# Attention, gated feed-forward and adaptive layer norm on one core: scores with keys on partitions, no row maximum, token-major projections, one pool layout

## Chip, cores, metric

One core of one Trainium2 chip. The time is the device time of one execution in microseconds (us), the median of several. A core has five engines that matter here: TensorE (PE; its weight loads, PEld, overlap its matmuls), VectorE (DVE), ScalarE (ACT), GpSimd (POOL, used here to issue transfers) and SyncE (SP, which issues most DMA transfers). SBUF is the memory that holds the tiles, PSUM the one that matmul results go to.

## The reference, cut to what matters

```python
S, D, Hq, Hkv, Dh, W, F = 2048, 1024, 32, 4, 128, 512, 3584       # batch 1, bfloat16
mod = (silu(c) @ w_mod).reshape(1, 6, 1, -1)                      # sa ca ga sb cb gb
h = layernorm(x) * (1 + ca) + sa
q = (h @ wq) per head;  k, v = last W rows of the caches, each shared by 8 heads
p = softmax(q @ k.T * Dh ** -0.5)                                 # 2048 x 512, per head
x = x + ga * ((p @ v), heads side by side) @ wo
h = layernorm(x) * (1 + cb) + sb
x = x + gb * ((silu(h @ w_gate) * (h @ w_up)) @ w_down)
```

The tokens are worked on in 4 chunks of 512. With 32 heads this makes 128 "heads" (a head of a chunk). Counted in matmuls with a moving operand of 512 columns, the reference needs 1024 for q, 512 for scores, 512 for p @ v, 1024 for wo and 2688 for the feed-forward part: 5760 in all.

## The kernel before

It puts queries on partitions for the scores, so that the row maximum and the row sum are reductions along the free axis. Then P must be transposed for p @ v; that is done by matmuls with a diagonal of the reciprocal sums. The residual x is kept feature-major (`xT`), so the final output is transposed back. The parts that the change touches, with cuts:

```python
def emit_q(g):                       # 8 matmuls, then qT (128 x 512) copied by ScalarE
    ...
def emit_s(g, qt):                   # qt: four blocks of 128 queries
    s_ps = aps_s.tile([P, W], FP32, name="s_ps", tag="s_ps")
    nc.tensor.matmul(s_ps, lhsT=st[g]["qT"][:, qsl], rhs=kT[:, kv, :], start=True, stop=True)
def emit_max(g, qt):
    nc.vector.tensor_reduce(out=mx, in_=s_ps, axis=AX.X, op=ALU.max)
    nc.vector.tensor_scalar(out=nmx, in0=mx, scalar1=-scale, scalar2=None, op0=ALU.mult)
def emit_exp(g, qt):
    nc.scalar.activation(out=p_sb, in_=s_ps, func=ACT.Exp, bias=st[g]["nmx"][qt],
                         scale=scale, accum_out=ssum)
def emit_recip_dg(g, qt):
    nc.vector.reciprocal(out=rs, in_=ssum)
    nc.vector.tensor_scalar(out=dg, in0=ident, scalar1=rs, scalar2=None, op0=ALU.mult)
def emit_T(g, qt):                   # P transposed and normalised by matmuls with dg
    for j in range(WT):
        nc.tensor.matmul(pT_ps[:, j, :], lhsT=p_sb[:, j * P:(j + 1) * P], rhs=dg, ...)
    (nc.vector.tensor_copy or nc.scalar.copy)(out=pT4[:, qt, :, :], in_=pT_ps)
def emit_o(g):                       # 4 matmuls with v_sb, copied by VectorE
    ...
# output projection: for a column block of 128, 32 matmuls with wo as stationary operand
nc.tensor.matmul(a_ps, lhsT=wo_t[:, hh, :], rhs=oT_bufs[cc][hg][:, hi, :], ...)
# second layer norm, feature-major: sums over features by matmuls with ones
nc.tensor.matmul(ln_ps[:, 0, :], lhsT=ones_bf, rhs=srcT[:, dt, ssl], ...)
nc.tensor.matmul(ln_ps[:, 1, :], lhsT=ones_bf, rhs=xsq, ...)
nc.scalar.activation(out=var_all, in_=var_all, func=ACT.Ln)
nc.scalar.activation(out=rstd, in_=var_all, func=ACT.Exp, scale=-0.5)
# end of a chunk: xf (features on partitions) transposed to tokens, copied, stored
nc.tensor.transpose(o_ps[:, dt, :], xf[:, dt, qt * P:(qt + 1) * P], ident)
```

The program text is not the order of execution: when it is built, a scheduler orders each engine's instructions and gives out the buffers.

## Time and profile before

| | before |
|---|---|
| median (lowest to highest), us | 1562.4 (1561.97 to 1566.34) |
| span of the profiled execution, us | 1565.7 |
| start to the first query projection | 65.2 |
| heads, output projection, second norm | 887.1 |
| feed-forward part and end | 613.4 |

The page's busy times of the kernel before (busy us, share of the span, instructions):

```profile
span 1565.7 us, 22987 instructions
## 1 busy us (share of the span) xinstructions
PE 1484.2 (95%) x8370; PEld 738.9 (47%) x8528; DVE 964.8 (62%) x2865; ACT 790.3 (50%) x1797; POOL 17.5 (1%) x31
```

A table of the kernel before by stretches of time: for each stretch its length, busy time and instruction count of each engine, the granted TensorE clock (1.00 is full), the DMA share and GB/s. The cuts are at the first query projection and the first gate matmul.

```profile
core 0: us, PE busy (x) PEld busy (x) DVE busy (x) ACT busy (x) POOL busy (x), PEclk, DMA share, GB/s
0.00:65.20 65.20, 41.41 (x337) 30.27 (x338) 41.82 (x130) 38.69 (x48) 3.47 (x9) 0.85 0.65 194
65.20:952.30 887.10, 851.29 (x5270) 437.78 (x5371) 732.44 (x2450) 661.87 (x1612) 5.29 (x6) 0.99 0.41 85
952.30:1565.70 613.40, 591.48 (x2768) 270.90 (x2821) 190.56 (x286) 89.75 (x139) 8.70 (x16) 0.99 0.57 148
```

TensorE is busy nearly all the time, but busy time alone does not say how many matmuls a head costs. The timeline does. Three successive p @ v groups of the kernel before (start, duration, engine, line, operation, output<-inputs, shape, count):

```profile
391.28 1.03 PE L413 MATMUL o_ps<-pT_6158,v_sb 128*128 128x512 bf16 x4
...
397.64 1.03 PE L413 MATMUL o_ps<-pT_6263,v_sb 128*128 128x512 bf16 x4
...
404.00 0.81 PE L413 MATMUL o_ps<-pT_6370,v_sb 128*128 128x512 bf16 x3
```

They start 6.36 us apart. A head has 24 matmuls of 512 columns (8 q, 4 scores, 4 p @ v, 8 wo) and 16 of 128 columns for the transposes. At 0.2162 us (39.8 us for 184 matmuls in a stretch of the feed-forward part) the 24 take 5.19 us; the transposes take the rest, 1.17 us. One matmul is listed with 379 ns while starts are 216 ns apart: the listed durations of neighbours overlap, so the distance between starts is what counts.

The costliest groups (line, engine, operation, shapes, count, busy us, mean ns, idle before):

```profile
L367 ACT ACTIVATE p_sb<-s_ps,nmx 128x512 bf16<-128x512 f32 x512 | 353.0, 699 | 4.4 <-DVE nmx L359 0.7 <-DVE rs L376 0.2
L357 DVE TENSOR_REDUCE mx<-s_ps 128x1 f32<-128x512 f32 x512 | 337.4, 682 | 19.0 <-PE s_ps L350 15.7 <-PE q_ps L334 0.2
...
L399 PE MATMUL pT_ps<-dg,p_sb 128*128 128x128 bf16 x2048 | 182.1, 218 | 12.9 <-ACT pT_8030 L404 2.4 <-ACT pT_11517 L404 2.4 <-ACT pT_872 L404 0.7
```

The exponentials and the row maxima look most expensive. They lie on engines with room, except among the heads before the output projection begins (65 to 268 us). One slice, in the form of the table above:

```profile
160.00:200.00 40.00, 36.57 (x247) 18.66 (x249) 38.76 (x142) 38.28 (x96) 0.00 (x0) 1.00 0.24 54
```

The third of the costliest lines is on the engine that binds.

### The profile page before, as it was taken

What the parts mean: (1) busy time and instruction counts of PE and PEld (TensorE: products, weight loads), DVE (VectorE), ACT (ScalarE), POOL (GpSimd) and SP (SyncE); (2) the same over time, 40 slices, a digit from 0 to 9 for tenths busy, and PEclk for the clock granted to TensorE, in tenths of its full rate; (3) what the DMA queues carried; (4) which work ended last, traced back from release to release, by engine and by line L of the source; (5) the groups of instructions that cost most, each with busy time, mean ns of one, the idle gap of its engine ahead of it and who ended that gap; (6) DMA issues with size and microseconds to landing.
All of it is one profiled execution on the core that took longest, in us unless ns stands there. A gap on an engine that the chain in (4) does not pass through costs nothing.

```text
span 1565.7 us, 22987 instructions
## 1 busy us (share of the span) xinstructions
PE 1484.2 (95%) x8370; PEld 738.9 (47%) x8528; DVE 964.8 (62%) x2865; ACT 790.3 (50%) x1797; POOL 17.5 (1%) x31
## 2 busy tenths in 40 slices
PE   6799999999999999999999999999999999999997
PEld 4544444555554555554555544444444444444443
DVE  5678999888888988888888715331333134213421
ACT  4658999777778877779777605110111011001100
POOL 0010000000000000000000000000000000000000
PEclk9799999999999999999999999999999999999998
DMA  8356222343534343434342477447645755574434
GB/s 272 62 167 133 54 55 48 68 95 72 97 73 84 68 95 68 95 68 89 74 95 48 81 135 208 162 161 141 168 143 166 138 158 161 155 142 154 141 71 98
DMA packets 452434, 178.71 MB, mean 114 GB/s; under 512 B 385760, under 2 KB 447200, under 8 KB 452320
## 3 DMA queue, kind: packets, MB, share of 16 engines
q1 hardware_dynamic: 448832, 164.64, 45.4%
q0 software_dynamic: 3488, 12.59, 2.3%
q8 instruction: 66, 1.08, 0.3%
q14 instruction: 48, 0.39, 0.1%
HBM read 173.02 MB, written 4.19 MB: 113 GB/s over the span
## 4 chain that ended last, share of the span: by engine, by line
PE 60%; issue 21%; ACT 10%; DVE 6%; DMA 1%; another core or an unknown queue 0%; POOL 0%; SPq 0%; ACTq 0%; POOLq 0%; DVEq 0%
PE a_ps L435 13%; PE q_ps L334 8%; PE d_ps L563 6%; PE g_ps L545 6%; PE u_ps L549 6%; PE s_ps L350 6%; PE pT_ps L399 6%; PE o_ps L413 5%; ACT p_sb L367 3%; DVE mx L357 2%; PE row_ps L221 2%; DMA xg_114<-in_A_x_dram 1%; PE modT_ps L230 1%; ACT qT L337 1%; DVE dg L386 1%
## 5 line engine op out<-in xcount | busy, mean ns | idle before, releaser
L367 ACT ACTIVATE p_sb<-s_ps,nmx 128x512 bf16<-128x512 f32 x512 | 353.0, 699 | 4.4 <-DVE nmx L359 0.7
L357 DVE TENSOR_REDUCE mx<-s_ps 128x1 f32<-128x512 f32 x512 | 337.4, 682 | 19.0 <-PE s_ps L350 15.7
L552 ACT ACTIVATE sig<-g_ps 128x512 bf16<-128x512 f32 x112 | 66.8, 597 | 444.0 <-PE g_ps L545 432.5
L399 PEld LDWEIGHTS <-p_sb 128*128 128x128 bf16 x2048 | 146.8, 97 | 124.4 <-issue 61.4
L563 PE MATMUL d_ps<-guT,wd 128*128 128x512 bf16 x879 | 195.3, 379 | 1.3 <-DMA wd<-in_B_w_down_dram 0.3
L399 PE MATMUL pT_ps<-dg,p_sb 128*128 128x128 bf16 x2048 | 182.1, 218 | 12.9 <-ACT pT_8030 L404 2.4
L350 PE MATMUL s_ps<-kT,qT 128*128 128x512 bf16 x506 | 160.7, 380 | 4.0 <-ACT p_sb L367 1.7
L435 PEld LDWEIGHTS <-wo_t 128*128 128x128 bf16 x1024 | 100.3, 98 | 122.4 <-issue 6.3
L563 PEld LDWEIGHTS <-wd 128*128 128x128 bf16 x896 | 87.5, 98 | 104.5 <-DMA wd<-in_B_w_down_dram 0.8
L549 PEld LDWEIGHTS <-wu 128*128 128x128 bf16 x896 | 87.4, 98 | 103.7 <-issue 0.8
L545 PEld LDWEIGHTS <-wg 128*128 128x128 bf16 x896 | 87.5, 98 | 103.2 <-issue 1.1
L565 DVE SCALAR_TENSOR_TENSOR xf<-d_ps,modT,xT 128x512 bf16<-128x512 f32 x32 | 24.0, 751 | 181.1 <-PE d_ps L563 181.1
L386 DVE TENSOR_SCALAR dg<-ident,rs 128x128 bf16<-128x128 bf16 x512 | 122.4, 252 | 6.1
L334 PEld LDWEIGHTS <-wq_h 128*128 128x128 bf16 x1024 | 90.4, 99 | 48.6 <-issue 4.2
L376 DVE RECIPROCAL rs<-ssum 128x1 f32<-128x1 f32 x512 | 81.5, 159 | 47.0 <-ACT p_sb L367 36.4
L367 ACT ACTIVATION_READ_ACCUMULATOR p_sb<-s_ps,nmx 128x1 f32 x512 | 109.3, 214 | 0.0
L413 PEld LDWEIGHTS <-v_sb 128*128 128x128 bf16 x512 | 48.8, 98 | 73.2 <-DVE nmx L359 11.0
L337 ACT CAST qT<-q_ps 128x512 bf16<-128x512 f32 x128 | 76.2, 595 | 4.8 <-PE q_ps L334 4.8
L350 PEld LDWEIGHTS <-qT 128*128 128x128 bf16 x512 | 49.5, 98 | 57.3 <-issue 3.6
L359 DVE TENSOR_SCALAR nmx<-mx 128x1 f32<-128x1 f32 x512 | 72.6, 142 | 0.0
L334 PE MATMUL q_ps<-h1T_106,wq_h 128*128 128x512 bf16 x241 | 71.4, 388 | 0.7 <-issue 0.2
L334 PE MATMUL q_ps<-h1T_109,wq_h 128*128 128x512 bf16 x242 | 68.8, 383 | 0.7
(815 smaller groups left out, 1910.6 us busy)
## 6 DMA issues: line engine op xcount, KB each, us to landing
wq_h<-in_A_wq_dram SPq DMA_DIRECT2D x128, 256.0 KB, 2.9
wo_t<-in_A_wo_dram SPq DMA_DIRECT2D x32, 1024.0 KB, 6.6
wg<-in_B_w_gate_dram SPq DMA_DIRECT2D x28, 1024.0 KB, 5.3
wu<-in_B_w_up_dram SPq DMA_DIRECT2D x28, 1024.0 KB, 7.2
wd<-in_B_w_down_dram SPq DMA_DIRECT2D x32, 896.0 KB, 5.8
wm_l<-in_w_mod_dram POOLq DMA_DIRECT2D x8, 1024.0 KB, 6.2
wm<-in_w_mod_dram SPq DMA_DIRECT2D x4, 1024.0 KB, 6.4
out_dram<-o_sb POOLq DMA_DIRECT2D x16, 256.0 KB, 2.3
```

The lines of the kernel that those rows point to most:

```text
L334: nc.tensor.matmul(q_ps, lhsT=wq_h[:, dt, :], rhs=h1T[cc][:, dt, :], start=(dt == 0), stop=(dt == DT - 1))
L337: nc.scalar.copy(out=qT, in_=q_ps)
L350: nc.tensor.matmul(s_ps, lhsT=st[g]["qT"][:, qsl], rhs=kT[:, kv, :], start=True, stop=True)
L357: nc.vector.tensor_reduce(out=mx, in_=s_ps, axis=AX.X, op=ALU.max)
L367: nc.scalar.activation(out=p_sb, in_=s_ps, func=ACT.Exp, bias=st[g]["nmx"][qt], scale=scale, accum_out=ssum)
L386: nc.vector.tensor_scalar(out=dg, in0=ident, scalar1=rs, scalar2=None, op0=ALU.mult)
L399: nc.tensor.matmul(pT_ps[:, j, :], lhsT=p_sb[:, j * P:(j + 1) * P], rhs=dg, start=True, stop=True)
L413: nc.tensor.matmul(o_ps, lhsT=v_sb[:, kv, j, :], rhs=pT4[:, :, j, :], start=(j == 0), stop=(j == WT - 1))
L435: nc.tensor.matmul(a_ps, lhsT=wo_t[:, hh, :], rhs=oT_bufs[cc][hg][:, hi, :], start=(hh == 0), stop=(hh == H - 1))
L545: nc.tensor.matmul(g_ps, lhsT=wg[:, dt, fi * P:(fi + 1) * P], rhs=hsrc[:, dt, :], start=(dt == 0), stop=(dt == DT - 1))
L549: nc.tensor.matmul(u_ps, lhsT=wu[:, dt, fi * P:(fi + 1) * P], rhs=hsrc[:, dt, :], start=(dt == 0), stop=(dt == DT - 1))
L563: nc.tensor.matmul(d_ps, lhsT=wd[:, f, :], rhs=guT[:, f, :], start=(f == 0), stop=(f == FT - 1))
```

## The change

Intent: put keys on partitions for the scores. P then comes out of the exponential in the layout that p @ v needs, and the transposes go. The row maximum would now be a reduction over partitions. It is left out; instead the chip computes a bound on the scores from norms of weights and keys, and if it is exceeded a branch at the end runs the old code ("general path"). Row sums come from adding the four key blocks on VectorE and one matmul with ones; the reciprocal is exp(-ln(sum)) on ScalarE, from one activation table set. The output and down projections have tokens on partitions, so the residual stays token-major and the last transposes go. Weights come in 512-column blocks. All SBUF tiles share a few pools. The core of the diff, with cuts:

```diff
+def emit_s(g):
+    p = blkA("pT", [P, WT, TCW])
+    for jj in range(WT // 2):
+        s_ps = big("s_ps")                                # 128 x 2 x 512, two PSUM banks
+        for i in range(2):
+            j = 2 * jj + i
+            nc.tensor.matmul(s_ps[:, i, :], lhsT=kT[:, kv, j * P:(j + 1) * P], rhs=qT[g], ...)
+        nc.scalar.activation(out=p[:, 2 * jj:2 * jj + 2, :], in_=s_ps, func=ACT.Exp, scale=scale)
+    nc.vector.tensor_tensor(out=a, in0=p[:, 0:2, :], in1=p[:, 2:4, :], op=ALU.add)
+    nc.vector.tensor_tensor(out=b, in0=a[:, 0, :], in1=a[:, 1, :], op=ALU.add)
+def emit_o(g):
+    nc.tensor.matmul(l_ps, lhsT=ones_bf, rhs=rec.pop(g), start=True, stop=True)
+    for j in range(WT):
+        nc.tensor.matmul(o_ps, lhsT=v_sb[:, kv, j, :], rhs=pT[g][:, j, :], ...)
+    nc.scalar.activation(out=r, in_=l_ps, func=ACT.Ln)
+    nc.scalar.activation(out=r, in_=r, func=ACT.Exp, scale=-1.0)
+    nc.vector.tensor_tensor(out=oT[(cc, hg)][:, hi, :], in0=o_ps, in1=r, op=ALU.mult)
+def emit_wo(cc, q, u):                                    # tokens on partitions, 8 heads at a time
+    nc.tensor.matmul(a_ps, lhsT=oT[(cc, 2 * q + i)][:, hh % 4, t * P:(t + 1) * P],
+                     rhs=wo_tiles[(cc, q, dh, i)][:, hh % 4, :], ...)
+def ln_stats(key, cc):                                    # per row of x, then 32 transposes to hT
+    for t in range(QT):
+        for i in range(DH):
+            nc.vector.bn_stats(out=st[:, i, :], in_=xt[cc * QT + t][:, i * 512:(i + 1) * 512])
+        nc.vector.bn_aggr(out=mv[:, t, :], in_=st)
+    nc.scalar.activation(out=rstd, in_=mv[:, :, 1], func=ACT.Ln, bias=eps_t)
+    nc.scalar.activation(out=rstd, in_=rstd, func=ACT.Exp, scale=-0.5)
+nc.scalar.preload_act_table_set("natural_log_exp_and_others")
+def bound_wq(hg, i, j): ...                               # 32 sums of squares over wq, one per head
+def bound_k(): ...
+def bound_final(): ...                                    # sets flag
+def emit_down(cc, dh, t):                                 # tokens on partitions, stored at once
+    nc.tensor.matmul(d_ps, lhsT=guT[(cc, f // 4)][:, f % 4, t * P:(t + 1) * P],
+                     rhs=wd_tiles[(cc, dh, f // 4)][:, f % 4, :], ...)
 ...
+    fast_path(tc, flag, *args)
+    over = nc.values_load(flag[0:1, 0:1], min_val=0, max_val=1)
+    with tc.If(over > 0):
+        general_path(tc, *args)
```

## The prediction

> **What bounds the kernel now.** TensorE. The page's busy table has PE at 95% of 1565.7 us, VectorE 62%, ScalarE 50%. In the feed-forward part (952 us to the end) a table by stretches gives 184 matmuls of 512 columns in 39.8 us: 0.2162 us each, with no gaps to speak of at granted clock 1.00. The Trainium skill (TensorE: Matmul & The Clock Gate, Back-to-back issue gap) gives 216 ns for one gap at 512 columns, which agrees; its "sustained 131 ns" does not. In attention the timeline shows a steady head every 6.36 us: 24 such matmuls (5.19 us) plus 16 transposing matmuls of 128 columns for P (about 1.17 us). Only the first 32 heads differ: before output-projection work arrives (65 to 268 us) VectorE (97% busy) and ScalarE (96%) bind, through the row maximum (682 ns each), exp with bias and accumulator read (699 + 214 ns), reciprocals, diagonal scalings and PSUM copies. The prologue ends at 65 us, where the first query projection starts.
>
> **Removed.** The 2048 transposing matmuls (about 1.17 us a head, 150 us of PE), 512 row maxima, negations, reciprocals, diagonals and 512 copies of transposed P. On the critical path that is the PE part, plus the vector/scalar excess of the early heads. The x-transposes of the prologue, the mean/variance matmuls with ones (some 27 us) and the final output transposes (about 14 us with their waits) go too.
>
> **Added.** One matmul a head for the row sums (0.216 us); 256 normalisation transposes (0.065 us, as the warm ones in the trace: 17 us); modulation columns (256 tiny matmuls, estimate 0.06 us) and 32 broadcast matmuls; VectorE sums of P, the bound check (32 products over weights, estimate 1.2 us each, hidden) and ScalarE's logarithm and exponential per head. ScalarE per head: two 1024-wide exps at about 1.02 us (the 1024-wide copy takes that) plus two of 0.6: 3.3 us. VectorE: 3 to 4.5 us. Both are under PE's 25 x 0.2162 = 5.41 us, so PE stays the limit.
>
> **Sum (us).** Prologue about 33 (6 MB at the 272 GB/s of the first slice, then modulation columns), was 65. Nine heads without projection work: limited by the chain scores, exps, sums, query copy, about 4.6 each plus the key bound: 46. 119 heads at 5.41, with the 1% that clock dips cost: 650. Modulation and broadcasts 12, normalisation transposes 13, stalls where eight statistics (0.66 us) jam VectorE and so exp, about 12. Projection left after the last head 16, last normalisation 7. Feed-forward 2688 x 0.2162 = 581, plus dips and waits for second-half down weights: 592. Tail with the branch 7. Total 1388.
>
> **Prediction: 1388 us, 1350 to 1430; faster by over 2% 0.97, within 2% 0.02, slower 0.01.**
>
> **What would show it.** Steady heads 5.4 us apart; first query projection near 33 us; VectorE and ScalarE under 80% throughout; feed-forward within 2% of 600 us; a few microseconds lost near each normalisation's statistics; no table loads between logarithm and exponential.
>
> **What would make it wrong.** Before, each Ln and the Exp after it cost a table load of 1.28 us; the skill (ScalarE: Activation LUTs, Table sets) says one set holds both, and the change preloads it. If loads nevertheless come twice a head, ScalarE needs 5.9 us a head and binds: about 1460. Larger stalls at normalisations or chained engine waits within a head (0.5 us a head is 64 us), or down weights arriving late, push it above 1430; a prologue overlapped better and no stalls give 1350.

## The result, and the profile after

| | before | after |
|---|---|---|
| median (lowest to highest), us | 1562.4 (1561.97 to 1566.34) | 1340.36 (1339.75 to 1341.4) |
| start to the first query projection | 65.2 | 26.9 |
| heads, output projection, second norm | 887.1 | 720.6 |
| feed-forward part and end | 613.4 | 591.3 |
| span of the profiled execution | 1565.7 | 1338.8 |

The ratio is 0.8562 (95% interval 0.8541 to 0.8583). The change was forecast in direction and kind; the time fell 48 us under the forecast and 10 us under the lower end of its range.

The busy line of the changed kernel:

```profile
span 1338.8 us, 15768 instructions
## 1 busy us (share of the span) xinstructions
PE 1302.6 (97%) x6332; PEld 604.0 (45%) x6457; DVE 670.0 (50%) x1208; ACT 486.4 (36%) x654; POOL 18.1 (1%) x38
```

The same table by stretches, cut at the same two events of the changed kernel:

```profile
core 0: us, PE busy (x) PEld busy (x) DVE busy (x) ACT busy (x) POOL busy (x), PEclk, DMA share, GB/s
0.00:26.90 26.90, 9.18 (x177) 7.77 (x178) 10.50 (x35) 4.93 (x9) 0.69 (x6) 0.84 0.94 298
26.90:747.50 720.60, 713.94 (x3497) 331.52 (x3565) 524.52 (x969) 410.25 (x528) 0.00 (x0) 0.99 0.36 117
747.50:1338.80 591.30, 579.52 (x2666) 264.67 (x2719) 135.02 (x205) 71.22 (x117) 17.41 (x32) 0.99 0.44 145
```

A steady head of the changed kernel on TensorE (timeline):

```profile
151.44 1.89 PE L945 MATMUL a_ps<-wo,oT 128*128 128x512 bf16 x8
153.17 0.38 PE L922 MATMUL l_ps<-psB,ones_bf 128*128 128x512 bf16 x1
153.38 1.03 PE L925 MATMUL o_ps<-pT,v_sb 128*128 128x512 bf16 x3
154.25 1.03 PE L903 MATMUL s_ps<-qT,kT 128*128 128x512 bf16 x4
155.11 1.89 PE L888 MATMUL q_ps<-hT,wq 128*128 128x512 bf16 x8
156.84 1.89 PE L945 MATMUL a_ps<-wo,oT 128*128 128x512 bf16 x8
```

From 151.44 to 156.84 are 5.40 us (three heads in a row: 5.395) for 8 + 1 + 4 + 4 + 8 = 25 matmuls, that is 0.2158 us each (the "x3" has lost one record). No line shows a wait. The list of TensorE's waits over the whole execution is short (who waited for whom, us in total, times, longest):

```profile
PE sil_ps L721 <- DVE sil_r L719: 8.0, 1, 8.0
PE k_ps L816 <- DMA k_ld<-in_A_k_cache_dram: 6.3, 1, 6.3
PE h_ps L780 <- DVE xn L771: 3.3, 1, 3.3
PE l_ps L922 <- DVE psB L912: 1.8, 1, 1.8
PE o_ps L925 <- DVE oT L930: 0.5, 1, 0.5
...
PE gu_ps L1022 <- DVE guT L1028: 0.2, 1, 0.2
```

The first three lie in the first 27 us, the fourth at 39 us. After that TensorE never waits longer than 0.5 us at a time. So the changed kernel, once it has begun, is a count of matmuls.

### The profile page after: what moved, and what is told of

It reads as the page before. It is cut to its first block, busy times and chain, and to the rows that moved or that the text cites. A ratio compares the mean times of both kernels' runs of the same rounds, so it can differ in the third digit from the quotient of the medians.

```text
span 1338.8 us, 15768 instructions
## 1 busy us (share of the span) xinstructions
PE 1302.6 (97%) x6332; PEld 604.0 (45%) x6457; DVE 670.0 (50%) x1208; ACT 486.4 (36%) x654; POOL 18.1 (1%) x38
## 4 chain that ended last, share of the span: by engine, by line
PE 61%; issue 33%; DVE 3%; SPq 1%; POOL 1%; DMA 1%; ACT 0%; POOLq 0%
PE q_ps L888 16%; PE a_ps L945 16%; PE o_ps L925 8%; PE s_ps L903 8%; PE gu_ps L1022 7%; PE d_ps L1039 3%; PE l_ps L922 2%; POOL out_dram L1047 1%; PE h_ps L780 1%; SPq L656 1%; DMA k_ld<-in_A_k_cache_dram 1%; DVE st L760 0%; PE mod_ps L730 0%; PE bc_ps L747 0%; ACT pT L905 0%
## 5 line engine op out<-in xcount | busy, mean ns | idle before, releaser
L905 ACT ACTIVATE pT<-s_ps 128x1024 bf16<-128x1024 f32 x256 | 247.9, 1021 | 14.4 <-PE s_ps L903 7.8
L888 PE MATMUL q_ps<-hT,wq 128*128 128x512 bf16 x993 | 243.0, 382 | 2.0 <-issue 0.2
L945 PE MATMUL a_ps<-wo,oT 128*128 128x512 bf16 x1008 | 239.8, 379 | 0.8
L1022 PE MATMUL gu_ps<-hT,wg 128*128 128x512 bf16 x878 | 210.1, 379 | 1.1 <-DVE guT L1028 0.2
L1022 PE MATMUL gu_ps<-hT,wu 128*128 128x512 bf16 x877 | 210.0, 379 | 1.0
L1039 PE MATMUL d_ps<-wd,guT 128*128 128x512 bf16 x878 | 193.3, 379 | 1.2 <-SPq L1093 0.2
L928 ACT ACTIVATE rinv<-l_ps 128x512 f32<-128x512 f32 x128 | 76.4, 597 | 273.7 <-PE l_ps L922 273.7
L888 PEld LDWEIGHTS <-wq 128*128 128x128 bf16 x1024 | 100.8, 99 | 122.6 <-issue 3.6
L945 PEld LDWEIGHTS <-oT 128*128 128x128 bf16 x1024 | 98.9, 98 | 114.5 <-issue 0.2
L925 PE MATMUL o_ps<-pT,v_sb 128*128 128x512 bf16 x498 | 131.4, 381 | 1.1 <-DVE oT L930 0.5
L903 PE MATMUL s_ps<-qT,kT 128*128 128x512 bf16 x504 | 130.5, 380 | 0.7 <-DVE qT L893 0.2
L929 ACT ACTIVATE rinv<-rinv 128x512 f32<-128x512 f32 x128 | 80.7, 631 | 4.0
```

Source lines behind the costliest of these rows:

```text
L888: nc.tensor.matmul(q_ps, lhsT=wq_tiles[(cc, h // 4, dt // 4)][:, dt % 4, (h % 4) * P:(h % 4 + 1) * P], rhs=hT[("h1", cc)][:, dt, :], start ...
L903: nc.tensor.matmul(s_ps[:, i, :], lhsT=kT[:, kv, j * P:(j + 1) * P], rhs=qT[g], start=True, stop=True)
L905: nc.scalar.activation(out=p[:, 2 * jj:2 * jj + 2, :], in_=s_ps, func=ACT.Exp, scale=scale)
L925: nc.tensor.matmul(o_ps, lhsT=v_sb[:, kv, j, :], rhs=pT[g][:, j, :], start=(j == 0), stop=(j == WT - 1))
L929: nc.scalar.activation(out=r, in_=r, func=ACT.Exp, scale=-1.0)
L945: nc.tensor.matmul(a_ps, lhsT=oT[(cc, 2 * q + i)][:, hh % 4, t * P:(t + 1) * P], rhs=wo_tiles[(cc, q, dh, i)][:, hh % 4, :], start=(hh == ...
```

## The experiments

Eleven runs follow, in three groups, each group on another chip. The first has the doubled row sum, the run without the preload, VectorE's forced order and the attention core alone; the second the unaltered changed kernel again, both forced orders, the run without the bound check and the later keys; the third the doubled exponentials, the later keys again and the two edits on them. The unaltered changed kernel was repeated in the second group only (1337.42 us, against 1340.36 us in the first measurement). So in the other two groups a difference of a few us from it is uncertain by some 3 us, and both distances are given.

### Is TensorE really the limit? Two row-sum matmuls per head

```diff
-nc.tensor.matmul(l_ps, lhsT=ones_bf, rhs=rec.pop(g), start=True, stop=True)
+rb = rec.pop(g)                                   # half_bf: all 0.5
+nc.tensor.matmul(l_ps, lhsT=half_bf, rhs=rb, start=True, stop=False)
+nc.tensor.matmul(l_ps, lhsT=half_bf, rhs=rb, start=False, stop=True)
```

> The changed kernel with one matmul more per head: the row sums come from two matmuls with halves in place of one with ones (same result). Theory A (TensorE sets the pace after the start, no slack at all): 128 more matmuls of 0.2158 us, 27.6 us longer, so about 1368 us. Theory B (the chain scores, exponential, sums, query copy sets the head's 5.4 us, and TensorE only happens to be nearly as long): under 8 us longer, about 1340 to 1348 us.

Measured: 1364.81 us, correct, ratio 0.8727 against 0.8562. That is 24 us over the first measurement of the changed kernel and 27 over its repeat in the second group; 27.6 were expected of theory A and under 8 of theory B. TensorE has no slack: a matmul more costs 0.19 to 0.21 us, close to its 0.2158.

### Have the others slack? Every exponential computed twice

```diff
-nc.scalar.activation(out=p[:, 2 * jj:2 * jj + 2, :], in_=s_ps, func=ACT.Exp, scale=scale)
+for _ in range(2):
+    nc.scalar.activation(out=p[:, 2 * jj:2 * jj + 2, :], in_=s_ps, func=ACT.Exp, scale=scale)
```

> The changed kernel with both exponentials of every head computed twice into the same tile (same result). ScalarE then has 3.17 + 1.95 = 5.1 us of work a head, under TensorE's 5.395, where the run without the preload had 5.7. Theory A (TensorE sets the pace and every other engine only has to stay under it): under 7 us longer, all of it among the first nine heads, which have no output projection and run at 3.7 to 4.4 us. Theory B (latency chains through ScalarE set the pace): 1 us a head or more, over 100 us longer.

Measured: 1344.97 us, ratio 0.8589: 4.6 us over the first measurement of the changed kernel, 7.6 over its repeat. The doubled work, 250 us of ScalarE, cost some 2 to 3% of itself. The stretch from 100 to 700 us, of this kernel:

```profile
100.00:700.00 600.00, 596.94 (x2897) 278.33 (x2954) 429.90 (x775) 542.69 (x661) 0.00 (x0) 1.00 0.29 96
```

and of the changed kernel:

```profile
100.00:700.00 600.00, 596.95 (x2868) 277.90 (x2925) 431.36 (x771) 343.86 (x443) 0.00 (x0) 1.00 0.29 95
```

ScalarE is busy 543 us of 600 instead of 344, and TensorE's busy time is the same to 0.01 us. Theory B, a pace set by latency through ScalarE, falls. The few us are lost in the early heads, as expected: the output projection begins at 80.7 us instead of 76.2, and the first gate matmul comes at 752.2 instead of 747.5, so nothing more is lost in between.

### What the preload is worth

```diff
-nc.scalar.preload_act_table_set("natural_log_exp_and_others")
```

> The changed kernel without the preload of the activation table set that holds both the exponential and the logarithm. If the loads then come twice a head, as they do around every logarithm of the kernel before, ScalarE needs 3.24 us (two exponentials of 0.97, 0.60, 0.63 as the trace has them) plus 2 x 1.28 = 5.8 us a head against TensorE's 5.4: 128 heads x 0.4 to 0.6 us more, 1390 to 1470 us. If one set is chosen that holds both without the preload: 1340 us and no more table loads than now.

Measured: 1395.49 us, ratio 0.8919, so 55 us longer than the changed kernel. ScalarE's groups of this kernel:

```profile
L904 ACT ACTIVATE pT<-s_ps 128x1024 bf16<-128x1024 f32 x256 | 245.5, 1010 | 5.1 <-PE s_ps L902 5.1
L927 ACT ACT_TABLE_LOAD x126 | 161.7, 1283 | 2.2
L928 ACT ACT_TABLE_LOAD x126 | 161.7, 1283 | 2.2
```

The loads do come twice a head, once for the logarithm (L927) and once for the exponential after it (L928); with the preload the whole execution has only five. The Trainium skill (ScalarE: Activation LUTs, Table sets: the hidden batching unit) says that a logarithm followed by an exponential needs one load because one set holds both. That came true only with the set chosen by hand. The stretch from 300 to 400 us:

```profile
300.00:400.00 100.00, 98.59 (x491) 45.31 (x490) 58.82 (x105) 95.20 (x103) 0.00 (x0) 0.98 0.26 85
```

ScalarE is busy 95 to 99% in every such stretch from 100 to 700 us, and TensorE's longest waits are now for query copies (16.0 us in 19 waits, by its list of waits). Together with the run before: at 4.9 us of ScalarE per head (542.69 of 600 us) nothing happens after the early heads, at 5.7 it binds. TensorE's 5.4 lies between. My forecast for this case, "about 1460", was 65 us too high: 48 of them are the base that it was added to, the other 17 the addition itself, 72 us forecast and 55 measured.

### Why did the normalisations cost nothing? VectorE in the order of the program text

The prediction allowed for stalls where the eight row statistics of a normalisation jam VectorE. The trace of the changed kernel shows them thinly spread. The rows of the third chunk are x_97 to x_100. In the view of the statistics' line (count, shortest/median/longest ns, first and last start in us) the first start of each belongs to the normalisation before attention, the last to the one after it:

```profile
L760 DVE BATCH_NORM_STATS2 st<-x_97 x4: 681/690/695, 242.3 to 592.5; 128x6 f32<-128x512 bf16 x4
L760 DVE BATCH_NORM_STATS2 st<-x_98 x4: 640/688/694, 248.3 to 597.9; 128x6 f32<-128x512 bf16 x4
L760 DVE BATCH_NORM_STATS2 st<-x_99 x4: 677/689/695, 256.5 to 603.3; 128x6 f32<-128x512 bf16 x4
L760 DVE BATCH_NORM_STATS2 st<-x_100 x4: 633/685/696, 264.6 to 608.7; 128x6 f32<-128x512 bf16 x4
```

Those before attention start at 242, 248, 256 and 265 us: over four heads and more, where the text has all of them in one. From 240 to 270 us VectorE is 97% busy (29.15 of 30 us), against 76% from 100 to 200 us, and yet the scores of the heads stay 5.40 us apart: the spread statistics take up nearly all the room that VectorE has. The experiment forces the text's order on VectorE, by edges in the issue order that wait for nothing:

```diff
 def ln_stats(key, cc):
+    with issue_after(last psB):                   # statistics follow this head's row-sum add
         ... 8 bn_stats, 4 bn_aggr; last = the last bn_aggr
 def emit_s(g):
+    with issue_after(last):                       # the next head's first add follows them all
         nc.vector.tensor_tensor(out=a, in0=p[:, 0:2, :], in1=p[:, 2:4, :], op=ALU.add)
```

> The changed kernel with the order on VectorE forced as the program text has it: the eight row statistics and four aggregates of a normalisation (about 6 us) stand together between two heads, for the six normalisations within the heads. My prediction took this order for granted. Theory A (the stalls I allowed for did not come because the compiled order spreads these statistics over many heads): six bursts of 2 to 5 us of TensorE idle, 12 to 30 us longer, 1352 to 1370 us. Theory B (the buffers absorb a 6 us burst, the allowance was wrong in itself): under 5 us longer.

Measured: 1341.97 us, ratio 0.8582 against 0.8562: 1.6 us over the first measurement of the changed kernel, 4.6 over its repeat; neither ran in this group. Theory A in this form falls. The timeline of one burst in this kernel (VectorE's burst and the scores around it):

```profile
263.01 1.87 DVE L766 BATCH_NORM_STATS2 st<-x 128x6 f32<-128x512 bf16 x3
...
264.26 1.03 PE L910 MATMUL s_ps<-qT,kT 128*128 128x512 bf16 x4
...
264.89 1.02 ACT L912 ACTIVATE pT<-s_ps 128x1024 bf16<-128x1024 f32 x1
...
268.80 0.30 ACT L770 ACTIVATE rstd<-mv,eps_t 128x4 f32<-128x4 f32 x1 [2.88 <-DVE mv L768]
...
270.23 1.03 PE L910 MATMUL s_ps<-qT,kT 128*128 128x512 bf16 x4
```

The burst lasts from 263.0 to 268.8. The scores before and after it are 5.97 us apart instead of 5.40: this burst costs 0.6 us. One reason can be read here: the scheduler, free on ScalarE, had put the next head's first exponential (264.89) ahead of the norm's logarithm (268.80), which has to wait for all statistics.

### ScalarE in that order as well

```diff
+with issue_after(this head's last exponential):   # on ScalarE
     nc.scalar.activation(out=rstd, in_=mv[:, :, 1], func=ACT.Ln, bias=eps_t)
     rs_i = nc.scalar.activation(out=rstd, in_=rstd, func=ACT.Exp, scale=-0.5)
+with issue_after(rs_i):
     ... the logarithm of the row sums, and the next head's two exponentials
```

> As the burst of statistics on VectorE, which cost under 2 us in all, and now ScalarE's order forced too, as the program text has it: the logarithm and exponential for the normalisation's scale stand ahead of the next head's logarithm and exponentials, so ScalarE, first in first out, waits for all the statistics. This is the whole order that my prediction assumed. Theory A (what saved the stalls is the compiled order, ScalarE's rather than VectorE's): six stalls of about 5 us, by the arithmetic of exponentials starting about 6 us late, so 20 to 35 us over the unaltered kernel of this batch. Theory B (slack and buffers absorb the burst whatever the order): under 6 us over it.

Measured: 1352.67 us (ratio 0.8634); the unaltered kernel of the same group took 1337.42 us (ratio 0.8547):

> The changed kernel unaltered, to be compared with the other runs on this chip: 1340 us (1336 to 1344).

So 15.2 us for six normalisations, 2.5 each on average. The same burst in this kernel:

```profile
271.15 0.67 DVE L964 COPY acc<-a_ps 128x512 f32<-128x512 f32 x1
...
271.88 1.89 PE L958 MATMUL a_ps<-wo,oT 128*128 128x512 bf16 x8 [1.69 <-DVE acc L964]
271.97 0.30 ACT L771 ACTIVATE rstd<-mv,eps_t 128x4 f32<-128x4 f32 x1 [7.37 <-DVE mv L768]
...
272.89 1.02 ACT L915 ACTIVATE pT<-s_ps 128x1024 bf16<-128x1024 f32 x1
```

ScalarE now stands idle 7.37 us. The next exponential begins at 272.89, 5.46 us after its scores (267.43); with VectorE alone forced it came 0.63 us after them (264.89 and 264.26), so it is 4.8 us late. TensorE loses only 1.69 us, waiting for a PSUM buffer that VectorE frees at the end of the burst, and 0.3 us more in the next head. Five of the six bursts have this wait of 1.69 us and cost about 2.1 us each. The first, at 144 us, waits 2.83 us, and the granted clock then falls to half for 3.4 us: it costs 4.7 us by the distance of the scores. That adds up to the 15.2.

The result lies between the two theories. In the order of the text there are stalls, and of the size that the prediction allowed for in sum (12 us forecast, 15 measured). In the order that was built there are none. VectorE's order alone costs little (0.6 us in the burst shown); most of the cost came only with ScalarE's as well. ScalarE's order alone was not run. My arithmetic per burst (5 us) was twice too large for five of the six: it chained the next query copy behind the next row-sum adds, while the scheduler put the copy first (271.86, the add at 275.57).

### The bound check

```diff
-at(4 * hg + 2 * i + j, bound_wq, hg, i, j) ...; at(5, bound_k); at(H + 2, bound_final)
-over = nc.values_load(flag[0:1, 0:1], min_val=0, max_val=1)
-with tc.If(over > 0):
-    general_path(tc, *args)
```

> The changed kernel without the bound check and without the branch and the general path behind it (same result for these inputs). If the check is hidden in VectorE's slack, as I predicted, only the branch at the end and the key bound among the first heads can be seen: 2 to 7 us shorter than the unaltered kernel of this batch. If it cost more than that (32 products of 1.2 us each, 39 us of VectorE), 10 us or more.

Measured: 1332.79 us (ratio 0.8505), 4.6 us less than the unaltered kernel of the group. From the last store's issue to the end are 4.1 us here (1326.90 to 1331.0) and 6.7 in the changed kernel (1332.06 to 1338.8), so some 2.5 us are the branch at the end. Where the other 2 lie is not shown: before the feed-forward part this run's profile is 1.4 us ahead of the unaltered kernel of its group (742.7 against 744.1), but two profiles of the unaltered kernel differ there by more (747.5 and 744.1). The Trainium skill (Runtime: NRT & Kernel Launch, Instruction fetch mechanics) says that a taken branch to a target outside the window of fetched instructions has to wait for a fetch. That fits: the skipped general path is long, and the changed kernel has two packets on an instruction queue (q8) in its last 11 us that this one has not. It was not tested further, so the fetch is a reading and not shown. The 39 us of products over the query weights (32 of 1.218 us) are hidden in VectorE's slack.

### The start

In the changed kernel TensorE waits 6.3 us for the keys, and does the modulation columns only then.

```diff
-kT = ...; for kv in range(Hkv): 4 transposes, 1 copy      # before the modulation columns
 ... modulation columns, first normalised chunk ...
 emit_q(0)
+kT = ...; for kv in range(Hkv): 4 transposes, 1 copy
```

> The changed kernel with the key transposes after the modulation columns and the first query projection in the program. In the trace TensorE waits 6.3 us for the keys' load before it may do the modulation columns, whose weights should have landed. If that order is what delays the start: first query projection at about 22 us in place of 26.9, and 3 to 5 us shorter than the unaltered kernel. If the loads themselves (8 MB at about 380 GB/s) set the start: under 1.5 us.

Measured: 1331.27 us (ratio 0.8501), 6.2 us less than the unaltered kernel of the group, more than the 3 to 5 expected. TensorE's first waits in this kernel:

```profile
PE sil_ps L721 <- DVE sil_r L719: 8.0, 1, 8.0
PE h_ps L780 <- DVE xn L771: 1.5, 1, 1.5
PE mod_ps L730 <- DMA wm<-in_w_mod_dram: 0.9, 1, 0.9
PE q_ps L882 <- DMA wq<-in_A_wq_dram: 0.5, 2, 0.4
```

The wait for the keys is gone and the first query projection starts at 18.6 us, earlier than the 22 expected. The order, not the sum of the loads, had delayed the start. In the changed kernel this stretch also ran at half the granted clock, but that is not the cause: the doubled row sum and VectorE's forced order had full clock there and began no sooner (27.2 and 27.7 us). This kernel, at 1331 us, beats both kernels of the comparison.

Two edits more were put on it: the key part of the check moved into heads 32 to 35, and the flag loaded as soon as it is known.

> The kernel with the key transposes later, again, as the base for the next: 1331 us (1328 to 1334).

> The kernel with the key transposes later, and two edits more: the key part of the bound check moved from the first heads to heads 32 to 35, where VectorE has room, in four pieces; and the flag for the branch loaded into the engines' registers as soon as it is known, not at the end. Without any check the kernel was 4.6 us shorter. If half of that is the flag's load at the end and the rest the key bound among the first heads: 2 to 4 us shorter than its base of this batch. If the branch itself is what costs: no gain.

Measured: base 1331.24 us, with the edits 1330.07 us (ratios 0.8505 and 0.8497). The gain of 1.2 us is less than expected and within the spread of the runs (1329.69 to 1331.74 against 1330.53 to 1332.23): inconclusive. From the last store to the end it is still 6.5 us, so the flag's load is not what the end waits for; the branch remains.

### The attention core alone, in the kernel before

```diff
-emit_s, emit_max, emit_exp, emit_recip_dg, emit_T, emit_o            # four blocks of queries
+emit_s, emit_o as in the change (keys on partitions, ones matmul, exp(-ln))
-nc.scalar.activation(out=sig_c, in_=cT, func=ACT.Sigmoid)            # start: same table set
+... exp, add 1, reciprocal; the table set preloaded
-PSUM: 3 + 3 + 2 banks      # projections, scores, transposes
+PSUM: 3 + 2 x 2 + 1 banks
```

> The kernel before with the new attention core alone (scores with keys on partitions, no row maximum, row sums by a ones matmul, the table set preloaded); start, projections, normalisations, feed-forward part and end as before; no bound check. Theory A (the time is a count of matmuls at 0.2158 us): start 65 us as before, heads and output projection 3200 x 0.2158 = 690 us plus some 60 us for normalisation and modulation matmuls and the early heads, feed-forward 612 us as before: about 1425 us, so some 60% of the whole gain. Rival (the gain lies mostly in the layouts and buffers of the rewrite, so the attention core alone still stalls): above 1470 us.

Measured: 1416.62 us, correct, ratio 0.9057. Its table by stretches, cut at the first query projection and the first gate matmul:

```profile
0.00:63.30 63.30, 39.35 (x336) 28.05 (x337) 41.66 (x132) 35.84 (x45) 3.48 (x9) 0.97 0.68 200
63.30:802.70 739.40, 733.87 (x3455) 336.95 (x3453) 296.13 (x530) 500.02 (x711) 5.30 (x6) 1.00 0.49 101
802.70:1415.70 613.00, 594.30 (x2822) 270.42 (x2820) 190.50 (x286) 89.67 (x139) 8.70 (x16) 0.99 0.57 148
```

Start and feed-forward part are as before (65.2 and 613.4), and the middle stretch fell from 887.1 to 739.4 us. So of the whole gain of 227 us between the two profiled executions, the attention core alone brings 148 to 150 us. By the tables, the rewrite of the rest brings 36 us at the start (63.3 to 26.9), 19 us in the middle (739.4 to 720.6: normalisation) and 22 us in the feed-forward part (no output transposes). The rival, that the layouts do most of it, falls. The reasons in brackets (normalisation, output transposes) are read from the code and not tested; for the second, the trace of this run has 12.9 us of waits before the output transposes. Nor is the 148 a count of matmuls alone. The transposes less the new ones matmul are 128 x (1.17 - 0.22) = 122 us. Of the other 26, some 16 lie before the output projection begins: that stretch fell from 203 us (65.2 to 268.5) to 155 (63.3 to 218.0) for 34 heads, where the matmuls explain 33 of the 49. There VectorE had been up to 97% busy, and its work in the middle fell by 60%, from 732 to 296 us. So the lighter VectorE and ScalarE are likely to count there, as the prediction said ("the vector/scalar excess of the early heads"); they were not tested apart.

## Why the prediction was wrong

The forecast as a sum, against the timeline of the changed kernel (us):

| term | forecast | measured | read from |
|---|---|---|---|
| start | 33 | 26.9 | first query projection |
| nine heads without output projection | 46 | 41.8 | 26.9 to 73.1, less 4.3 of modulation |
| 119 heads | 650 | 642 | 119 x 5.395 |
| modulation within the heads | 12 | 10.2 | 4 x 1.73 and 4 x 0.81 |
| six sets of normalisation transposes | 13 | 10.7 | 6 x 1.78 |
| stalls at the statistics | 12 | 0 | no such wait in the list |
| output projection after the last head | 16 | 15.8 | the rest up to 747.5 |
| last normalisation | 7 | 1.8 | 32 transposes, 761.6 to 763.4 |
| feed-forward matmuls | 592 | 581.0 | 747.5 to 1330.3, less 1.8 |
| end | 7 | 8.5 | 1330.3 to 1338.8 |
| sum | 1388 | 1338.7 | span 1338.8 |

The row of the output projection is what is left over, so the sum closes by construction. But the 72 matmuls that belong there take 15.5 us at 0.2158, so no stall is hidden in it.

**Right.** TensorE was the limit and stayed it (the doubled row sum). What was removed on the critical path was the transposes, 1.17 us a head, and some 16 us among the early heads; the steady head came out at 5.40 us, as forecast (5.41). ScalarE stayed under it (the doubled exponentials), and so did VectorE. But "under 80% throughout" was wrong for VectorE: 97% from 240 to 270 us, without cost. The table loads were the hazard that I named, and the preload avoids it (the run without). The bound check and its branch cost 4.6 us.

**Wrong: the allowances.** The step that failed leads from the count to the time: the prediction took it that a normalisation's statistics would hold up VectorE and the exponentials, and TensorE behind them, and that the clock dips of the kernel before would come again. About 36 of the 48 us are four items that were added to a sound count of matmuls and did not come: "stalls where eight statistics jam VectorE and so exp, about 12" (0); "with the 1% that clock dips cost" on the heads (8 us, one of them the slightly faster matmul; after 42 us the granted clock of the changed kernel does not fall before the last matmul); "last normalisation 7" (1.8, because TensorE went on with gate matmuls while the statistics ran); "plus dips and waits for second-half down weights: 592" (581.0 is 2688 x 0.2162 and nothing more; the longest wait at a down matmul was 0.2 us). For the first, the runs show why: with these instructions of both engines held to the text's order the six normalisations within the heads cost 15 us; the order that was built costs nothing. I had taken the text for the order of execution. For the clock the cause stays open (below).

**Wrong: the start and the small matmuls.** The start was forecast 6 us too long. The last load that it waits for came at 21.7 us, near the 22 that 6 MB at 272 GB/s make. What followed took 5.2 us instead of 11: the 128 modulation columns took 3.4 us (23.5 to 26.9), 0.027 us each instead of my 0.06. The normalisation transposes took 0.056 us each instead of 0.065. The Trainium skill (TensorE: Matmul & The Clock Gate, Wait — 56ns, not 53.3ns?) gives 25 ns as the least distance of small matmuls and 55.6 ns for 128 columns; the trace agrees with both (0.81 us for 32 columns within the heads are 25 ns each; the 27 ns above are at half the granted clock), and I should have used them.

**Wrong: the range.** Its lower end, 1350, was described as "a prologue overlapped better and no stalls". Taking the stall and clock items out of the sum (12, 8, 5, 11) gives 1352 before any of the start's 6 us and the early heads' 4. So the range did not reach the case in which the allowances are empty. An optimistic end should have been the bare count.

**Open.** The clock. In the kernel before the granted clock fell to half for 3.4 us four times between 100 and 1300 us, at 503, 714, 950 and 1261 us (its runs with a mean clock of 0.993 to 0.994 took 1559 to 1562 us, those with 0.982 to 0.986 1566 to 1571 us); the changed kernel's fell only before 42 us and after the last matmul. Those four falls follow waits of TensorE (2.35, 2.35, 1.51 after two shorter ones, 2.98 us), and so does the one in the run with both orders forced (2.83 us). But the length of the wait does not settle it: five waits of 1.69 us in that run and one of 2.04 us in the kernel before have no fall after them, a wait of 1.84 us had one in one profile of the changed kernel and none in the other, and waits of 5.9 and 6.5 us for the keys had none in two runs (doubled row sum, VectorE's order). What sets the falls was not tested.

## What to carry to other kernels

Count the matmuls, multiply by the measured distance between starts, and check that each other engine's work per step is below it; here the forecast without its allowances would have been within 1%. Do not add allowances for jams to such a count before having looked at the order that is really built: here a scheduler that moved statistics and exponentials between steps hid work that takes 5.8 us in one piece, longer than a whole step of 5.4. When an activation chain needs two functions, look for table loads in the trace: choosing one common set by hand was worth 55 us here.

## What the Trainium skill lacked or had wrong

- TensorE: Matmul & The Clock Gate, Back-to-back issue gap: it gives a sustained 131 ns for 512 columns and 81 ns for 128 with weight loads between. Here a stream of load and matmul pairs runs at 215.8 ns for 512 columns and 55.6 ns for the normalisation transposes of 128; the page's "isolated" figures (about 216 and 56) are the ones that hold in a stream.
- ScalarE: Activation LUTs, Table sets: it does not say that the set with both functions must be preloaded; without that 126 + 126 loads came, where the changed kernel has five loads in all.
- ScalarE: Activation LUTs, What ACT_TABLE_LOAD costs: 1283 ns for a load agrees to the digit. The further 1380 ns of drain for each switch does not appear: in the run without the preload the next activation begins 0.01 us after the load ends (309.75 + 1.28, then 311.04), and the load itself 0.02 us after the exponentials before it, and a head with two loads needs 5.7 us in all.
- No page that I read says how far a program's work is moved from the order of its text on each engine: statistics over four heads and more here; with the text's order forced the kernel took 15 us longer.
- Runtime: NRT & Kernel Launch, Instruction fetch mechanics: it names the stall after a far branch but gives no time. Skipping a long block at the end of the kernel cost 2.5 us here, whether the flag was loaded early or late; that this is that stall was not tested.
